# Later places in TensorE's order for the two products that spread v's maxima, and a place behind v's low parts for GpSimd's low parts of u

## The chip, the core and the metric

The kernel runs on one core of one Trainium2 chip. A core has five engines with a queue each, worked through in order: TensorE (PE, matrix products into PSUM), VectorE (DVE), ScalarE (ACT), GpSimd (POOL) and SyncE (SP), which issues the DMAs here. The metric is the device time of one execution, in microseconds (us).

## What is computed

Windowed attention, and behind it a mixing over tokens and over channels, on 8 batches of 8 heads, 576 tokens and 64 dimensions per head (512 channels):

```python
scores = scale * q @ k.T + bias          # only 0 <= i - j < 128
attn = exp(scores - max) / sum
x = attn @ v                             # heads side by side: (8, 576, 512)
theta = x @ w_theta
y = w_tok_r @ (x * cos(theta)) + w_tok_i @ (x * sin(theta))
u = x + y
out = u + maximum(u @ w_ch, 0)
```

## The kernel before, in words

Single numbers are carried as a high and a low part of smaller width, and a product is made of three products of parts. In TensorE's work this shows as groups like `wtk_hi,z_hi`, `wtk_lo,z_hi`, `wtk_hi,z_lo`.

**Two batches at a time.** After a start-up of its own, a loop over the batches runs `attend` for batch b+1 while the token mixing of batch b (`mix`, a generator that makes three products of 288 columns per step) fills TensorE in between; then `turn` transposes the new batch's x, multiplies by w_theta and makes z (cosine and sine), beside the channel products (`channels`) of batch b. `attend` is worked in four *slots* per batch, one per pair of heads; in the texts here slot 0 is the first. A slot p computes the scores of the next pair (`scores`, tiles `s_ps` and one `mm`; L394 on VectorE adds the bias and takes the extreme, L397 on ScalarE is the exponential), transposes the exponentials of its own pair (`flip`, four banks 0 to 3; tile `t_ps`; ScalarE copies the high part, L409, VectorE the low part, L410), multiplies them by v for its first head and its second (`values`, tile `acc`), and divides (`finish`, L444 to L447, into `x_sb`). Banks 0 and 2 are flipped at the slot's head, 1 and 3 behind the scores. STEPS (L33) gives the numbers of mixing steps put between them: 7, 7, 6, 3 in slot 0, 3, 4, 6, 4 in slot 1 and 3, 4, 6, 3 in slots 2 and 3.

**Buffers.** `t_ps` has two PSUM buffers, so flip 1 takes that of flip 0 and flip 3 that of flip 2, once ScalarE and VectorE have read them. `s_ps` and `acc` have one, `mm` has three, shared by the mixing, channel and theta products, the first score tile and the products of the change. `vh`/`vl` have two each.

**v's scales.** v is scaled by a power of two for each head before it is split. Heads are taken in groups of four. In an even slot `measure` takes the group's absolute maxima per partition (L239, then a floor, L241, into `peak`). In the next, odd, slot they are spread over the partitions: `spread_first` has TensorE transpose `peak` (L76), VectorE takes the maximum (L251) and makes a diagonal of it (L253); `spread_scales` has TensorE multiply ones by the diagonal (L71, `mm<-fixed`), and VectorE makes the scales (L127, L129; for every second group also the batch's scale, L268 to L270 and L134). `split_values` then uses a scale for a head: ScalarE makes `vh` (L329), GpSimd writes its ones column (L330), VectorE makes `vl` (L331). This is called by `ready` for the heads of the next pair, once behind the first head's `finish` and once behind the second's. `prepare` splits the next but one pair's q and k there too (`qh` L310, `ql` L311, `kh` L313 and `kl` on GpSimd L315) and issues the loads of the pair after that; `qr`, which they load, has one buffer, so its load follows `ql`.

**u's parts.** When a part of the mixing ends (eight parts per batch: a half of the tokens by a quarter of the channels), VectorE adds it to x (L567), ScalarE rounds it to `u_hi` (L569) and GpSimd makes the rest, `u_lo` (L570). The channel products read both.

**What sets the order.** From the main loop on, TensorE's instructions keep the order in which the program writes them (`pinned`). The other engines' orders are worked out ahead of time by the framework's scheduler, from its own estimate of times and from priorities; `high_priority(250)` moves the instructions of a block forward, and `issue_after(ins)` puts instructions behind another in that order. A semaphore wait is only put in where data or a buffer asks for it.

Of the kernel before, what the change touches and what calls it, by code (L numbers as in the profile page):

```python
# [34 lines left out]
GROUP = 4  # L35
# [11 lines left out]
def attn_moe_kernel(ctx: ExitStack, tc: tile.TileContext, qt, kt, vx, wth, wtok, wch, band, out):  # L47
# [19 lines left out]

    pinned = []

# [248 lines left out]
    def split_values(n):  # L318

        if n < H:  # L320
            if n % GROUP == 0:
                group_v[n // GROUP] = load_plain(n // GROUP)
            return (group_v[n // GROUP][:, n % GROUP],), None
        vb, scale = group_v[n // GROUP]
        k = n % GROUP
        v, vs = vb[:, k, :, :64], scale[:, k:k + 1]
        vh = vp.tile([128, 5, 65], F16, name="vh")
        vl = vp.tile([128, 5, 64], F16, name="vl")
        nc.scalar.activation(vh[:, :, :64], v, AF.Copy, scale=vs)  # L329
        nc.gpsimd.memset(vh[:, :, 64:], 1.0)  # L330
        nc.vector.scalar_tensor_tensor(out=vl, in0=v, scalar=vs, in1=vh[:, :, :64], op0=ALU.mult, op1=ALU.subtract)  # L331
        return (vh, vl), vs

# [84 lines left out]
    class Head:  # L418
# [5 lines left out]
        def ready(self):  # L424
            self.v, self.vs = split_values(self.n)

# [117 lines left out]
    def mix(st):  # L544
# [8 lines left out]
        def part(g, ks):  # L553
# [12 lines left out]
            if ks[-1] == 8:  # L566
                nc.vector.scalar_tensor_tensor(out=xtf[:, m, cs], in0=y_ps[:, :HALF], scalar=st["back"],  # L567
                                               in1=xtf[:, m, cs], op0=ALU.mult, op1=ALU.add)
                nc.scalar.copy(u_hi[:, m, cs], xtf[:, m, cs])  # L569
                nc.gpsimd.tensor_tensor(out=u_lo[:, m, cs], in0=xtf[:, m, cs], in1=u_hi[:, m, cs].bitcast(F32),  # L570
                                        op=ALU.subtract)
                yield
# [46 lines left out]
    def attend(b, x_sb, mixing, chans, first, behind):  # L619

        for g in range(H // 2):
# [18 lines left out]
            scores(SCORES[0])  # L640
            scores(SCORES[1])
            if scaled:
                with tc.high_priority(FINISH):
                    spread_first(scaled)
            step(mixing, steps[1])
            pair.flip(1)
            pair.flip(3)
            if scaled:
                with tc.high_priority(FINISH):
                    spread_scales(scaled)  # L650
            step(mixing, steps[2])
            one.values()
            with tc.high_priority(FINISH):
                done = one.finish(x_sb)
            scores(SCORES[2])
            with tc.issue_after(done.ins):
                if new is not None:
# [8 lines left out]
            if new is not None:  # L666
                with tc.issue_after(done.ins):
                    new.heads[1].ready()
                    if measured:
                        measure(measured)  # L670

    def start(x_sb, load):
# [140 lines left out]
```

## Time and profile before

| | us |
|---|---|
| three runs | 765.84, 770.71, 2267.97 (median 770.71) |
| the profiled execution | 762.94 |
| its span, first to last instruction | 761.2 |
| mean granted TensorE clock | 0.943 of full |

In the profile, a line such as L71 is that of the kernel above; since helpers record all matrix products, L71 holds nearly all of them, and L76 all transposes: the tiles tell them apart. A row of the timeline gives start, duration, engine, line, operation, output and inputs, shape and number, and in brackets the idle time of that engine just before with what ended it. A row of windows gives, per engine, busy time and number of instructions, then the granted clock of TensorE, the share of the DMA engines and GB/s. Matrix products overlap in the pipeline: the pace is read from start to start.

### The profile page before, as it was taken

To read this page: it belongs to the slowest core of one execution; us is meant where nothing else is said; L and a number is where in the kernel's file an instruction comes from. 1 tells how busy PE (TensorE), PEld (TensorE's weight loads), DVE (VectorE), ACT (ScalarE), POOL (GpSimd) and SP (SyncE) were. 2 spreads that over 40 slices of the span, in tenths; PEclk is the share of its full clock that TensorE was granted. 3 is DMA by queue.
4 is the path that set the end of the run, shared out by engine and by line. 5 is a ranking of instruction groups with operands and counts; after the bars stand their busy time and mean duration, and the time that the engine had idled before them with its cause. 6 is when DMAs were issued, how large, how long until landed. Compare 5 with 4: busy or idle time off the path is not lost.

```text
span 761.2 us, 16035 instructions
## 1 busy us (share of the span) xinstructions
PE 686.3 (90%) x6221; PEld 584.1 (77%) x6221; DVE 565.1 (74%) x1528; ACT 503.6 (66%) x988; POOL 156.5 (21%) x200
## 2 busy tenths in 40 slices
PE   4888797999979999799979999799989999799998
PEld 2567675789868888689868798688867898689887
DVE  6988756885887867886787867786687867874722
ACT  5988386576965678475966578565975579554910
POOL 2211321221221302221212302222211212210220
PEclk9886598999989999999999999899999999999999
DMA  9455200332021310232011220222012220000001
GB/s 304 149 182 181 78 1 1 89 85 64 24 67 33 93 57 14 67 103 68 24 53 47 81 65 17 67 76 88 23 42 66 75 71 17 18 9 33 25 9 55
DMA packets 32620, 49.86 MB, mean 66 GB/s; under 512 B 5664, under 2 KB 22048, under 8 KB 32544
## 3 DMA queue, kind: packets, MB, share of 16 engines
q1 hardware_dynamic: 32544, 48.84, 21.0%
q8 instruction: 49, 0.80, 0.4%
q14 instruction: 27, 0.22, 0.1%
HBM read 39.39 MB, written 9.44 MB: 64 GB/s over the span
## 4 chain that ended last, share of the span: by engine, by line
PE 44%; DVE 28%; ACT 21%; issue 3%; DMA 3%; SPq 1%; POOL 0%; DVEq 0%; ACTq 0%; POOLq 0%
PE mm L71 29%; PE acc L71 6%; PE t_ps L76 5%; DVE pt L410 4%; PE s_ps L71 3%; ACT g L509 3%; ACT z_hi L460 3%; ACT g L508 2%; DVE ql L311 2%; DVE peak L239 2%; ACT xtf L482 2%; DVE s_sb L394 2%; DVE g L513 2%; ACT x_hi L480 2%; DVE f L513 1%
## 5 line engine op out<-in xcount | busy, mean ns | idle before, releaser
L71 PE MATMUL mm<-wtk_hi,z_lo 128*128 128x288 f16 x576 | 169.9, 295 | 5.6 <-DVE z_lo L461 5.0
L71 PE MATMUL mm<-wtk_hi,z_hi 128*128 128x288 f16 x576 | 170.5, 296 | 3.8 <-ACT z_hi L460 3.8
L71 PE MATMUL mm<-wtk_lo,z_hi 128*128 128x288 f16 x576 | 170.0, 295 | 0.0
L397 ACT ACTIVATE s_sb<-s_sb,fixed 128x256 f32<-128x256 f32 (+1 forms) x256 | 104.1, 470 | 56.7 <-DVE fixed L394 56.7
L71 PEld LDWEIGHTS <-z_hi 128*128 128x128 f16 x1152 | 113.0, 102 | 36.6 <-ACT z_hi L460 4.4
L570 POOL TENSOR_TENSOR u_lo<-xtf,u_hi 128x288 fp32r<-128x288 f32 x64 | 50.6, 797 | 278.7 <-ACT u_hi L569 262.6
L410 DVE SCALAR_TENSOR_TENSOR pt<-t_ps,pt 128x512 f16<-128x512 f32 x112 | 74.7, 684 | 28.1 <-ACT pt L409 28.0
L394 DVE CUSTOM_DVE_ANT_0 s_sb<-s_ps,bands 128x256 f32<-128x256 f32 (+1 forms) x256 | 84.7, 384 | 1.2 <-PE s_ps L71 1.2
L71 PEld LDWEIGHTS <-z_lo 128*128 128x128 f16 x576 | 58.0, 101 | 26.1 <-DVE z_lo L461 8.6
L409 ACT ACTIVATE pt<-t_ps 128x512 f16<-128x512 f32 x112 | 61.6, 585 | 20.8 <-PE t_ps L76 20.8
L76 PE MATMUL t_ps<-fixed,s_sb 128*128 128x128 f32 x448 | 65.2, 286 | 4.5 <-ACT s_sb L397 2.3
L315 POOL TENSOR_TENSOR kl<-kr,kh 128x576 fp32r<-128x576 f32 x32 | 55.8, 1742 | 65.4 <-ACT kh L313 65.4
L569 ACT CAST u_hi<-xtf 128x288 fp32r<-128x288 f32 x64 | 27.2, 426 | 54.2 <-DVE xtf L567 53.7
L76 PEld LDWEIGHTS t_ps<-fixed,s_sb 128*128 128x128 f32 x448 | 55.0, 149 | 7.5 <-ACT s_sb L397 2.9
L71 PE MATMUL acc<-vh,pt 128*128 128x65 f16 x1008 | 55.8, 194 | 0.0
L71 PEld LDWEIGHTS <-pt 128*128 128x128 f16 x1512 | 52.8, 98 | 3.3
L71 PE MATMUL acc<-vl,pt 128*128 128x64 f16 x504 | 52.3, 193 | 0.0
L461 POOL TENSOR_TENSOR z_lo<-g,z_hi 128x512 f16<-128x512 f32 x16 | 19.1, 1196 | 156.1 <-ACT z_hi L460 156.1
L71 PE MATMUL s_ps<-kh,qh 64*128 64x256 f32 (+1 forms) x256 | 44.0, 341 | 7.3 <-DVE fixed L394 7.3
L71 PE MATMUL mm<-wth_hi,x_hi 128*128 128x512 f32 x160 | 48.0, 423 | 2.5 <-ACT x_hi L480 1.6
L567 DVE SCALAR_TENSOR_TENSOR xtf<-mm,fixed,xtf 128x288 f32<-128x288 f32 x64 | 32.3, 514 | 21.8 <-PE mm L71 21.2
L71 PE MATMUL mm<-u_hi,wch_hi 128*128 128x288 f32 x256 | 47.3, 307 | 0.0
(141 smaller groups left out, 1546.6 us busy)
## 6 DMA issues: line engine op xcount, KB each, us to landing
vb<-in_vx_dram SPq DMA_DIRECT2D x16, 650.0 KB, 5.2
kr<-in_kt_dram SPq DMA_DIRECT2D x32, 288.0 KB, 3.2
out_dram<-xtf SPq DMA_DIRECT2D x64, 144.0 KB, 1.8
qr<-in_qt_dram SPq DMA_DIRECT2D x32, 144.0 KB, 2.7
qr<-in_qt_dram SPq DMA_DIRECT2D x32, 128.0 KB, 2.8
xtf<-in_wtok_dram SPq DMA_DIRECT2D x4, 576.0 KB, 4.7
u_hi<-in_wtok_dram SPq DMA_DIRECT2D x3, 576.0 KB, 4.5
u_lo<-in_wtok_dram SPq DMA_DIRECT2D x2, 576.0 KB, 6.0
```

Of the source, the lines that this page charges most:

```text
L71: ins = nc.tensor.matmul(*args, **kw)
L76: ins = nc.tensor.transpose(*args)
L315: nc.gpsimd.tensor_tensor(out=kl, in0=kr, in1=kh.bitcast(F32), op=ALU.subtract)
L394: nc.vector.tensor_tensor_reduce(out=sb, in0=ps, in1=bias, scale=2.0 ** -(2 * self.p % H + 1), scalar=3.0e38, op0=ALU.add, op1=ALU.min, ac ...
L397: self.exp = nc.scalar.activation(sb, sb, AF.Exp, bias=least, scale=-1.0)
L409: nc.scalar.activation(pt[:, 0], t_ps, AF.Copy, scale=2.0 ** PEXP)
L410: nc.vector.scalar_tensor_tensor(out=pt[:, 1], in0=t_ps, scalar=2.0 ** PEXP, in1=pt[:, 0], op0=ALU.mult, op1=ALU.subtract)
L460: st["turned"] = nc.scalar.copy(z_hi[:, c, :], z)
L509: nc.scalar.activation(g[:n], g[:n], AF.Sin, bias=halfpi[:n], scale=-RAD)
L567: nc.vector.scalar_tensor_tensor(out=xtf[:, m, cs], in0=y_ps[:, :HALF], scalar=st["back"], in1=xtf[:, m, cs], op0=ALU.mult, op1=ALU.add)
L569: nc.scalar.copy(u_hi[:, m, cs], xtf[:, m, cs])
L570: nc.gpsimd.tensor_tensor(out=u_lo[:, m, cs], in0=xtf[:, m, cs], in1=u_hi[:, m, cs].bitcast(F32), op=ALU.subtract)
```

## The change

`spread_first` moves from behind the second scores to behind the third group of mixing steps, directly ahead of the first head's values, and `spread_scales` from behind the flips 1 and 3 to behind the slot's last scores. `ready` hands back the instruction that makes `vl`, and the subtraction that makes `u_lo` is kept in a list for all batches but the last and written at the end of the slot, in a block behind the second head's `vl`. No instruction is added or removed.

```diff
-    pinned = []
+    pinned, lows = [], []
...
-        nc.vector.scalar_tensor_tensor(out=vl, in0=v, scalar=vs, in1=vh[:, :, :64], op0=ALU.mult, op1=ALU.subtract)
-        return (vh, vl), vs
+        low = nc.vector.scalar_tensor_tensor(out=vl, in0=v, scalar=vs, in1=vh[:, :, :64], op0=ALU.mult,
+                                             op1=ALU.subtract)
+        return (vh, vl), vs, low
...
         def ready(self):
-            self.v, self.vs = split_values(self.n)
+            self.v, self.vs, low = split_values(self.n)
+            return low
...
                 nc.scalar.copy(u_hi[:, m, cs], xtf[:, m, cs])
-                nc.gpsimd.tensor_tensor(out=u_lo[:, m, cs], in0=xtf[:, m, cs], in1=u_hi[:, m, cs].bitcast(F32),
-                                        op=ALU.subtract)
+                def low(m=m, cs=cs):
+                    nc.gpsimd.tensor_tensor(out=u_lo[:, m, cs], in0=xtf[:, m, cs], in1=u_hi[:, m, cs].bitcast(F32),
+                                            op=ALU.subtract)
+
+                if st["b"] + 1 < B:
+                    lows.append(low)
+                else:
+                    low()
...
             scores(SCORES[1])
+            step(mixing, steps[1])
+            pair.flip(1)
+            pair.flip(3)
+            step(mixing, steps[2])
             if scaled:
                 with tc.high_priority(FINISH):
                     spread_first(scaled)
-            step(mixing, steps[1])
-            pair.flip(1)
-            pair.flip(3)
-            if scaled:
-                with tc.high_priority(FINISH):
-                    spread_scales(scaled)
-            step(mixing, steps[2])
             one.values()
             with tc.high_priority(FINISH):
                 done = one.finish(x_sb)
             scores(SCORES[2])
+            if scaled:
+                with tc.high_priority(FINISH):
+                    spread_scales(scaled)
             with tc.issue_after(done.ins):
                 if new is not None:
                     new.heads[0].ready()
...
                 with tc.issue_after(done.ins):
-                    new.heads[1].ready()
+                    done = new.heads[1].ready()
+                    with tc.issue_after(done.ins):
+                        for low in lows:
+                            low()
                     if measured:
                         measure(measured)
+            else:
+                for low in lows:
+                    low()
+            lows.clear()
```

The rows below are the program's order on an engine, with the semaphores that an instruction waits for in brackets (named for the engine that raises them). TensorE in a slot 1 of the steady state, before, from the last scores of the next pair's second group (`peak_108` is the tile of maxima, `z_hi` the mixing's weights):

```order
L71 MATMUL s_ps<-kh,ql 128x256 x2
L71 MATMUL s_ps<-kl,qh 128x256 x2
L76 MATMUL mm<-fixed,peak_108 128x128 [waits DVE_49]
L71 LDWEIGHTS z_hi
L71 MATMUL mm<-wtk_hi,z_hi 128x288
L71 LDWEIGHTS z_hi
L71 MATMUL mm<-wtk_lo,z_hi 128x288
L71 LDWEIGHTS z_lo
L71 MATMUL mm<-wtk_hi,z_lo 128x288
```

The transpose of the maxima stands directly behind the scores, ahead of the mixing. There, now, the slot runs on into the mixing and the flips of banks 1 and 3 (`t_ps`):

```order
L71 LDWEIGHTS z_lo
L71 MATMUL mm<-wtk_hi,z_lo 128x288
L76 MATMUL t_ps<-fixed,s_sb_3804 128x128 [waits DVE_49]
L76 MATMUL t_ps<-fixed,s_sb_3804 128x128
L76 MATMUL t_ps<-fixed,s_sb_3804 128x128 [waits Activation_49]
L76 MATMUL t_ps<-fixed,s_sb_3804 128x128
L76 MATMUL t_ps<-fixed,s_sb_3805 128x128 [waits DVE_49,PE_49]
L76 MATMUL t_ps<-fixed,s_sb_3805 128x128
L76 MATMUL t_ps<-fixed,s_sb_3805 128x128 [waits Activation_49]
L76 MATMUL t_ps<-fixed,s_sb_3805 128x128
L71 LDWEIGHTS z_hi
```

The transpose is gone from here, and the flips themselves now wait for VectorE, which they did not have to do behind a transpose that waited for it. It now stands ahead of the first head's values, and the product with the diagonal behind the last scores:

```order
L71 LDWEIGHTS z_lo
L71 MATMUL mm<-wtk_hi,z_lo 128x288
L76 MATMUL mm<-fixed,peak_108 128x128 [waits DVE_49]
L71 LDWEIGHTS pt [waits Activation_49]
L71 MATMUL acc<-vh,pt 128x65 [waits Pool_49]
L71 LDWEIGHTS pt
```

It is the last TensorE instruction ahead of `acc`. Further on in the same slot, behind the second head's score products:

```order
L71 MATMUL s_ps<-kh,ql 128x256 x2
L71 MATMUL s_ps<-kl,qh 128x256 x2
L71 MATMUL mm<-fixed 128x4 [waits DVE_49]
L71 LDWEIGHTS z_hi
L71 MATMUL mm<-wtk_hi,z_hi 128x288
L71 LDWEIGHTS z_hi
```

Both keep their wait for VectorE. ScalarE at the end of the same slot, before and then now (`vh` is v's high part for the next pair, `pt` the high part of a flip of the next slot):

```order
L329 ACTIVATE vh<-vb,fixed 128x5x64 [waits PE_49,DMAHW3_49,Activation_49,Pool_49]
L313 CAST kh<-kr 128x576 [waits DMAHW2_49,PE_49]
L397 ACTIVATE s_sb_4046<-s_sb_4046,fixed 128x256 [waits DVE_49]
L397 ACTIVATE s_sb_4047<-s_sb_4047,fixed 128x256 [waits DVE_49]
L397 ACTIVATE s_sb_4046<-s_sb_4046,fixed 128x256 [waits DVE_49]
L329 ACTIVATE vh<-vb,fixed 128x5x64 [waits PE_49,Activation_49,Pool_49]
L397 ACTIVATE s_sb_4047<-s_sb_4047,fixed 128x256 [waits DVE_49]
L409 ACTIVATE pt<-t_ps 128x512 [waits PE_49]
L409 ACTIVATE pt<-t_ps 128x512 [waits PE_49,Activation_49]
L310 ACTIVATE qh<-qr,fixed 128x640 [waits DMAHW6_49,DMAHW5_49,DMAHW4_49]
```

There one `vh` stood ahead of `kh` and the other among the exponentials. Now:

```order
L313 CAST kh<-kr 128x576 [waits DMAHW2_49,PE_49]
L398 ACTIVATE s_sb_4036<-s_sb_4036,fixed 128x256 [waits DVE_49]
L398 ACTIVATE s_sb_4037<-s_sb_4037,fixed 128x256 [waits DVE_49]
L398 ACTIVATE s_sb_4036<-s_sb_4036,fixed 128x256 [waits DVE_49]
L398 ACTIVATE s_sb_4037<-s_sb_4037,fixed 128x256 [waits DVE_49]
L329 ACTIVATE vh<-vb,fixed 128x5x64 [waits DVE_49,DMAHW3_49,Activation_49,Pool_49]
L329 ACTIVATE vh<-vb,fixed 128x5x64 [waits PE_49,Activation_49,Pool_49]
L410 ACTIVATE pt<-t_ps 128x512 [waits PE_49]
L310 ACTIVATE qh<-qr,fixed 128x640 [waits DMAHW6_49,DMAHW5_49,DMAHW4_49]
L410 ACTIVATE pt<-t_ps 128x512 [waits PE_49,Activation_49]
```

Both `vh` stand together now behind the four exponentials, the first of them waits for VectorE's scale, and `qh` stands between the two `pt`. VectorE at the end of slot 3, before and then now (the row with `x_hi` belongs to `turn`):

```order
L567 SCALAR_TENSOR_TENSOR xtf<-mm,fixed,xtf 128x288 [waits PE_49]
L593 SCALAR_TENSOR_TENSOR xtf<-mm,xtf 128x288 [waits PE_49,Pool_49]
L444 TENSOR_SCALAR fixed<-acc,fixed 128x5 [waits PE_49]
L446 RECIPROCAL fixed<-fixed 128x5 [waits DVE_49]
L447 TENSOR_TENSOR x_sb<-acc,fixed 128x5x64 [waits DVE_49]
L331 SCALAR_TENSOR_TENSOR vl<-vb,fixed,vh 128x320 [waits Activation_49]
L593 SCALAR_TENSOR_TENSOR xtf<-mm,xtf 128x288 [waits PE_49,Pool_49]
L476 TENSOR_TENSOR x_hi<-t_ps,x_hi 128x4x64 [waits Activation_49]
```

The second head's end stood behind the two `xtf` sums. Now:

```order
L569 SCALAR_TENSOR_TENSOR xtf<-mm,fixed,xtf 128x288 [waits PE_49]
L129 TENSOR_SCALAR fixed<-fixed 128x4 [waits DVE_49]
L601 SCALAR_TENSOR_TENSOR xtf<-mm,xtf 128x288 [waits PE_49,Pool_49]
L331 SCALAR_TENSOR_TENSOR vl<-vb,fixed,vh 128x320 [waits Activation_49]
L446 TENSOR_SCALAR fixed<-acc,fixed 128x5 [waits PE_49]
L448 RECIPROCAL fixed<-fixed 128x5 [waits DVE_49]
L449 TENSOR_TENSOR x_sb<-acc,fixed 128x5x64 [waits DVE_49]
L331 SCALAR_TENSOR_TENSOR vl<-vb,fixed,vh 128x320 [waits Activation_49]
L601 SCALAR_TENSOR_TENSOR xtf<-mm,xtf 128x288 [waits PE_49,Pool_49]
L478 TENSOR_TENSOR x_hi<-t_ps,x_hi 128x4x64 [waits Activation_49]
```

A `vl` and the last step of the scale (L129) have come in ahead of the second head's end, the three rows of L444 to L447 (now L446 to L449). GpSimd at the end of slot 3, before and then now (`kl` is k's low part):

```order
L570 TENSOR_TENSOR u_lo<-xtf,u_hi 128x288 [waits Activation_49] x2
L330 MEMSET vh 128x5 [waits PE_49,Pool_49]
L315 TENSOR_TENSOR kl<-kr,kh 128x576 [waits DMAHW1_49,PE_49,Activation_49]
L330 MEMSET vh 128x5 [waits PE_49,Pool_49]
L570 TENSOR_TENSOR u_lo<-xtf,u_hi 128x288 [waits Activation_49]
```

The last `u_lo` of the batch closed the row. Now:

```order
L573 TENSOR_TENSOR u_lo<-xtf,u_hi 128x288 [waits Activation_49] x2
L330 MEMSET vh 128x5 [waits PE_49,Pool_49]
L315 TENSOR_TENSOR kl<-kr,kh 128x576 [waits DMAHW1_49,PE_49,Activation_49]
L573 TENSOR_TENSOR u_lo<-xtf,u_hi 128x288 [waits Activation_49]
L330 MEMSET vh 128x5 [waits PE_49,Pool_49]
```

The last `u_lo` stands ahead of the memset instead of behind it. And GpSimd in the slots 0 and 1 that follow, before and then now:

```order
L570 TENSOR_TENSOR u_lo<-xtf,u_hi 128x288 [waits Activation_49,Pool_49]
L570 TENSOR_TENSOR u_lo<-xtf,u_hi 128x288 [waits Activation_49]
L330 MEMSET vh 128x5 [waits PE_49]
L315 TENSOR_TENSOR kl<-kr,kh 128x576 [waits DMAHW7_49,PE_49,Activation_49]
L330 MEMSET vh 128x5 [waits PE_49]
L570 TENSOR_TENSOR u_lo<-xtf,u_hi 128x288 [waits Activation_49]
L330 MEMSET vh 128x5 [waits PE_49,Pool_49]
L570 TENSOR_TENSOR u_lo<-xtf,u_hi 128x288 [waits Activation_49]
L315 TENSOR_TENSOR kl<-kr,kh 128x576 [waits DMAHW2_49,PE_49,Activation_49]
```

Two `u_lo` lead, and one follows each of two memsets. Now:

```order
L573 TENSOR_TENSOR u_lo<-xtf,u_hi 128x288 [waits Activation_49,Pool_49]
L573 TENSOR_TENSOR u_lo<-xtf,u_hi 128x288 [waits Activation_49]
L330 MEMSET vh 128x5 [waits PE_49]
L315 TENSOR_TENSOR kl<-kr,kh 128x576 [waits DMAHW7_49,PE_49,Activation_49]
L330 MEMSET vh 128x5 [waits PE_49,Pool_49]
L573 TENSOR_TENSOR u_lo<-xtf,u_hi 128x288 [waits Activation_49]
L330 MEMSET vh 128x5 [waits PE_49,Pool_49]
L573 TENSOR_TENSOR u_lo<-xtf,u_hi 128x288 [waits Activation_49]
L315 TENSOR_TENSOR kl<-kr,kh 128x576 [waits DMAHW2_49,PE_49,Activation_49]
```

These stand as they stood, and `u_lo` waits for ScalarE (and the first for GpSimd itself), not for VectorE.

More of the change, by code (lines that the diff above doesn't have):

```diff
@@ L322, in split_values @@
                 group_v[n // GROUP] = load_plain(n // GROUP)
-            return (group_v[n // GROUP][:, n % GROUP],), None
+            return (group_v[n // GROUP][:, n % GROUP],), None, None
         vb, scale = group_v[n // GROUP]
```

## The prediction

> **What bounds the kernel now.** I read the page first, then the waits, the timeline of one batch, and busy time by windows. From the page, the span and the engines' busy shares:
>
> ```profile
> span 761.2 us, 16035 instructions
> PE 686.3 (90%) x6221; PEld 584.1 (77%) x6221; DVE 565.1 (74%) x1528; ACT 503.6 (66%) x988; POOL 156.5 (21%) x200
> ```
>
> TensorE is nearly always busy, so what counts is why it idles and how fast it is clocked. From the waits (us in total, times, longest):
>
> ```profile
> PE mm L76 <- DVE peak L241: 30.1, 13, 3.3
> PE s_ps L71 <- DVE fixed L394: 7.3, 8, 1.7
> ```
>
> The largest wait is the first of the two products to be moved: 13 times TensorE stands at the transpose of the maxima until VectorE has measured them. The timeline at the start of slot 1 (I number a batch's slots 0 to 3; 1 and 3 spread maxima), then the stall in the first such slot and in a slot 3:
>
> ```profile
> 309.23 0.28 PE L71 MATMUL s_ps<-kl,qh 64*128 64x256 f32 x2
> 309.30 0.54 DVE L331 SCALAR_TENSOR_TENSOR vl<-vb,fixed,vh 128x320 f16<-128x320 f32 x1
> 309.76 1.48 DVE L239 TENSOR_REDUCE peak<-vb 128x4 f32<-128x1280 f32 x1
> 311.16 0.68 DVE L410 SCALAR_TENSOR_TENSOR pt<-t_ps,pt 128x512 f16<-128x512 f32 x1
> 312.03 0.69 DVE L410 SCALAR_TENSOR_TENSOR pt<-t_ps,pt 128x512 f16<-128x512 f32 x1
> 312.63 0.16 DVE L241 TENSOR_SCALAR peak<-peak 128x4 f32<-128x4 f32 x1
> 312.85 0.33 PE L76 MATMUL mm<-fixed,peak 128*128 128x128 f32 x1 [3.34 <-DVE peak L241]
> ...
> 139.09 0.47 PE L76 MATMUL mm<-fixed,peak 128*128 128x128 f32 x1 [1.85 <-DVE peak L241]
> ...
> 341.47 0.33 PE L76 MATMUL mm<-fixed,peak 128*128 128x128 f32 x1 [1.30 <-DVE peak L241]
> ```
>
> Of the 13 waits, six are of the 3.34 kind (20.0 us), one is the 1.85, six are of slot 3 (30.1 - 20.0 - 1.85 = 8.2). Behind each slot-1 stall the granted clock (the column after POOL) is halved; I took the seven windows in which it stood at half, first, third and sum shown, and one behind a slot-3 stall:
>
> ```profile
> 139.00:142.40 3.40, 3.31 (x14) 2.21 (x15) 1.98 (x12) 1.92 (x5) 0.79 (x1) 0.50 0.29 107
> ...
> 313.10:316.50 3.40, 3.40 (x17) 2.42 (x16) 1.56 (x9) 1.85 (x5) 0.80 (x1) 0.50 0.16 55
> ...
> sum 30.00, PE 27.22 PEld 19.90 DVE 15.72 ACT 16.74 POOL 5.32; mean PE 3.89 PEld 2.84 DVE 2.25 ACT 2.39 POOL 0.76
> ...
> 341.50:344.90 3.40, 3.40 (x30) 2.97 (x31) 2.57 (x13) 2.65 (x7) 0.16 (x1) 1.00 0.29 106
> ```
>
> 27.22 us of TensorE work at half clock would take half as long at full clock: 13.6 us lost, 1.7 of it in the first slot 1 (half of 3.31), 2.0 in each of the other six. So the stalls and their clock cost 43.7 us, the most that this change could return.
>
> **The change: part one, the products.** Nothing is added or removed. In a scaled slot the transpose moves behind 12 mixing products, eight flips and up to 18 more mixing products; the product with the diagonal moves behind the first head's values and the last scores.
>
> *Start of slot 1.* TensorE is free at 309.23 + 0.28 = 309.51. The pace of mixing products and the flips of a slot that does not spread:
>
> ```profile
> 338.45 0.29 PE L71 MATMUL mm<-wtk_hi,z_hi 128*128 128x288 f16 x1
> 338.57 0.29 PE L71 MATMUL mm<-wtk_lo,z_hi 128*128 128x288 f16 x1
> ...
> 328.28 1.04 PE L76 MATMUL t_ps<-fixed,s_sb 128*128 128x128 f32 x8
> 331.36 0.19 PE L71 MATMUL acc<-vh,pt 128*128 128x65 f16 x1
> ```
>
> Twelve at 0.12 end at 310.98. Then comes the wait that stood hidden under the old one: flip 1 takes the buffer of flip 0, which VectorE's low part reads until 311.84, and flip 3 that of flip 2, until 312.72. So 0.86 us and, four transposes (0.45) later, 0.43: 1.29 instead of 3.34, a gain of 2.05. In the first slot 1 the same steps find both parts done; 1.85 goes entirely.
>
> *Clock.* The 1.3 us left are no longer than the slot-3 stalls, behind which the clock is 1.00. I take the full 2.0 (1.7 in the first). The other end is 0, since 1.85 us did halve it.
>
> The Trainium skill (TensorE: Matmul & The Clock Gate, "What's actually happening") has the clock halve after at least one idle window of some 3.4 us. Here the halving after 1.85 us of idleness disagrees with that; by the page alone these stalls, all shorter, would not be what halves it, and the sum would lose its clock term.
>
> *Middle of slot 1.* Flips and 18 products last 331.36 - 328.28 = 3.08, so the transpose comes at about 315.5 and the first head's values end at 316.5. The diagonal's product needs L251 and L253, which on VectorE now stand behind both low parts (0.68 each) and a part of u's columns:
>
> ```profile
> L567 DVE SCALAR_TENSOR_TENSOR xtf<-mm,fixed,xtf 128x288 f32<-128x288 f32 x64 | 32.3, 514 | 21.8 <-PE mm L71 21.2
> ...
> L251 DVE TENSOR_REDUCE fixed<-mm 128x1 f32<-128x128 f32 x15 | 4.3, 285 | 0.0
> ```
>
> I put the end of flip 3's low part at 316.2 to 316.3 (ScalarE makes its high part behind four exponentials), and then 0.51, 0.29 and as much again for L253: 317.3. TensorE reaches the product after the last scores, near 317.4. About level: I take no wait; ends 0 and 0.3 a batch.
>
> *End of slot 1.* The spread values now arrive late, so ScalarE's vh and VectorE's vl of the first head stand behind the second head, directly ahead of the low parts that release the next slot's flips; on ScalarE the second flip's high part now stands behind qh, which waits for its DMA. Against that, VectorE loses an idle time and a collision:
>
> ```profile
> 302.00:328.28 26.28, 22.20 (x263) 18.57 (x259) 22.43 (x66) 14.77 (x31) 6.55 (x10) 0.94 0.24 71
> ...
> 317.35 0.16 DVE L127 TENSOR_SCALAR fixed<-mm 128x4 int32<-128x4 int32 x1 [2.69 <-PE mm L71]
> 321.29 0.88 DVE L311 SCALAR_TENSOR_TENSOR ql<-qr,fixed,qh 128x640 fp32r<-128x640 f32 x1
> 322.08 1.70 DVE L331 SCALAR_TENSOR_TENSOR vl<-vb,fixed,vh 128x320 f16<-128x320 f32 x1
> ...
> 321.94 1.49 POOL L315 TENSOR_TENSOR kl<-kr,kh 128x576 fp32r<-128x576 f32 x1 [0.50 <-ACT kh L313]
> ...
> 305.10 2.03 DVE L311 SCALAR_TENSOR_TENSOR ql<-qr,fixed,qh 128x640 fp32r<-128x640 f32 x1
> ...
> 304.82 1.62 POOL L315 TENSOR_TENSOR kl<-kr,kh 128x576 fp32r<-128x576 f32 x1
> ```
>
> vl beside GpSimd's kl took 1.70 against 0.54 alone; ql begun before kl 0.88, begun after it 2.03. vl now stands clear of kl. But kh no longer waits behind vh, so kl can start about when ql does. If ql is first, VectorE runs 3.7 us earlier at the end of the slot and the next flips do not wait: the 2.05 and the clock's 1.7 to 2.0 are kept. If kl is first, ql loses 1.15, qh's DMA starts that much later, and the flips of slot 2 wait 1.15. My steps put the two within 0.1 us, less than their error, so I take the middle: 0.6 lost.
>
> The Trainium skill (SBUF — State Buffer, "Who interferes with whom") says that a VectorE instruction with two SBUF inputs and a GpSimd one that reads SBUF exclude each other for a whole instruction, whichever starts first; the rows of ql agree, and by it the loss is either nothing or the whole 1.15.
>
> *Slot 3.* TensorE is free 1.30 before 341.47, runs 12 products to 341.65, and the low parts of the flips were done at 340.46 and 341.34 (first two rows below). All of 8.2 is regained. But vl of the first head now stands ahead of the second head's end, which the next stage waits for:
>
> ```profile
> 339.77 0.69 DVE L410 SCALAR_TENSOR_TENSOR pt<-t_ps,pt 128x512 f16<-128x512 f32 x1
> ...
> 340.65 0.69 DVE L410 SCALAR_TENSOR_TENSOR pt<-t_ps,pt 128x512 f16<-128x512 f32 x1
> ...
> 351.57 0.41 ACT L569 CAST u_hi<-xtf 128x288 fp32r<-128x288 f32 x1
> ...
> 351.88 0.22 DVE L444 TENSOR_SCALAR fixed<-acc,fixed 128x5 f32<-128x5 f32 x1
> ...
> 352.36 0.49 DVE L447 TENSOR_TENSOR x_sb<-acc,fixed 128x320 f32<-128x320 f32 x1
> ...
> 353.35 0.60 PE L76 MATMUL t_ps<-fixed,x_sb 128*128 128x128 f32 x4
> ...
> 353.68 0.84 ACT L310 ACTIVATE qh<-qr,fixed 128x640 fp32r<-128x640 f32 x1 [1.16 <-DMA qr<-in_qt_dram]
> ...
> 380.56 0.30 PE L71 MATMUL mm<-wtk_hi,z_lo 128*128 128x288 f16 x1 [0.66 <-DVE z_lo L461]
> ```
>
> x_sb ended at 352.85, 0.5 ahead of TensorE; the head's end (L444) began at 351.88. Now vh starts behind u_hi on ScalarE, which ends about 0.5 before its old 351.98 (the queues ahead lost a vl), so vh is done near 352.1, vl near 352.6 (352.85 if it meets u_lo on GpSimd), and only then comes L444: 0.75 to 1.0 later, 0.25 to 0.5 of waiting. ScalarE also has one more vh, behind qh, ahead of x_hi, and that stage already ends with TensorE waiting 0.66 for it. I take 0.6 in each of six batches; ends 0 and 1.2.
>
> **Part two, GpSimd's low parts of u.** The instructions that the order shows carry no new wait: u_lo still waits for ScalarE alone and stands where it stood, but for one place in slot 3, where it goes ahead of a small memset. So vl of slot 0 will meet u_lo as before, and I cost this part at nothing. Ends: nothing, and 0.6 per batch if it did wait (vl of slot 0 back from 1.12 to 0.54):
>
> ```profile
> 303.27 1.55 POOL L570 TENSOR_TENSOR u_lo<-xtf,u_hi 128x288 fp32r<-128x288 f32 x2 [12.82 <-ACT u_hi L569]
> ...
> 304.05 1.12 DVE L331 SCALAR_TENSOR_TENSOR vl<-vb,fixed,vh 128x320 f16<-128x320 f32 x1
> ```
>
> SP's queue is not reordered; qr's loads follow ql, as said. The vectors of the first group and the last batch are untouched.
>
> **The sum,** against the profiled execution (762.9 us, span 761.2 and 1.7 around it): slot 1, six times 2.05 + 2.0 - 0.6 = 20.7; the first one 1.85 + 1.7 = 3.5; slot 3 gives 8.2 - 3.6 = 4.6. Together 28.8: 734. The runs shown, 765.8 and 770.7, lie 3 and 8 above the profiled one; I take the nearer and predict 737.
>
> **Rivals.**
> 1. *The clock stays gated.* 0.86 and 0.43 us of waiting in one stretch, added to a wait of s_ps before them (7.3 us in 8), might still halve it. Against: 1.00 behind 1.30. The clock term's 13.7 goes: 751. The page's rule gives the same time by another way: windows that these stalls do not cause stay. Chance 0.10.
> 2. *VectorE and ScalarE become the bound.* VectorE is busy 22.43 of 26.28 us in slots 0 and 1; my steps ask it for some 3.7 less. If kl is always first and qh's DMA holds back the high part, each batch keeps about 2.5 us less: 745 to 750. Chance 0.15.
> 3. *The waits re-form so far that little remains*, flips and the next stage both late: 755 to 768. Against: VectorE's idle 2.69 in the old slot shows room. Chance 0.11.
> 4. *GpSimd does wait as the words say:* six times 0.6 more, 733. The order speaks against it. Chance 0.06.
> 5. *Slower, by the diagonal's product.* TensorE's queue is fixed, so a late L253 stops everything. It decides once L253 lies some 5 us behind TensorE in slot 1 (28.8 over six), with the clock halved again: six times 7.5 against 28.8 is 16 slower, 782. My steps have them level. Chance 0.03.
>
> **How the numbers follow.** My forecast, 727 (kl second, no loss at the next stage) to 742, has 0.55. The range 726 to 753 holds it and rivals 1, 2 and 4 and leaves out rivals 3 and 5 and some of the tails, together under 0.2. A measurement of this kernel tells about 2%, here 15 us, from no change: faster needs less than 755. Forecast and rivals 1, 2, 4 are below it with small tails: 0.82; rival 3 and the tails 0.14; slower 0.04.
>
> **What would show it.** The wait of L76 for peak gone, TensorE's largest new waits at t_ps in slot 1 at about 0.9 and 0.4; no half-clock window in the steady batches; vl in slot 1 at 0.54; vl in slot 0 still near 1.12 with u_lo beside it; x_sb later against TensorE at the end of slot 3. A wait at the diagonal's product above 1 us, half-clock windows, or flips of slot 2 that wait over 1.2 would prove me wrong.

## The result, and the profile after

The changed kernel takes 732.1 us (median of four runs, 731.1 to 733.2) against 770.7: a ratio of 0.952, 95% interval 0.947 to 0.957. One run of the kernel before took 2268 us; the ratio and its interval leave it out. The profiled execution took 731.1 against 762.9, which is 31.8 less; 28.8 less had been forecast. From the page of the changed kernel, and its waits (us in total, times, longest), those of TensorE that the loop has:

```profile
span 729.2 us, 16045 instructions
PE 678.5 (93%) x6219; PEld 578.7 (79%) x6221; DVE 556.5 (76%) x1528; ACT 500.2 (69%) x988; POOL 155.9 (21%) x200
```

```profile
PE s_ps L71 <- DVE fixed L395: 7.3, 8, 1.7
PE t_ps L76 <- DVE pt L411: 5.6, 8, 0.8
PE mm L71 <- DVE z_lo L463: 5.0, 8, 0.7
...
PE t_ps L76 <- DVE peak L241: 2.2, 7, 0.3
```

The wait for the maxima, 30.1 us in 13 times before, is gone. In its place stand the two waits at t_ps, 7.8 together; those at s_ps and z_lo are old. The timeline of the steady slot 1, of the changed kernel (start, duration, engine, line):

```profile
299.52 1.48 DVE L239 TENSOR_REDUCE peak<-vb 128x4 f32<-128x1280 f32 x1
300.92 0.68 DVE L411 SCALAR_TENSOR_TENSOR pt<-t_ps,pt 128x512 f16<-128x512 f32 x1
...
301.65 0.66 PE L76 MATMUL t_ps<-fixed,s_sb 128*128 128x128 f32 x4 [0.80 <-DVE pt L411]
301.79 0.68 DVE L411 SCALAR_TENSOR_TENSOR pt<-t_ps,pt 128x512 f16<-128x512 f32 x1
302.62 0.63 PE L76 MATMUL t_ps<-fixed,s_sb 128*128 128x128 f32 x4 [0.31 <-DVE peak L241]
...
305.29 0.27 PE L76 MATMUL mm<-fixed,peak 128*128 128x128 f32 x1
...
307.21 0.38 PE L71 MATMUL mm<-fixed 128*128 128x4 f32 x2
...
307.64 0.88 DVE L311 SCALAR_TENSOR_TENSOR ql<-qr,fixed,qh 128x640 fp32r<-128x640 f32 x1
307.96 1.82 POOL L315 TENSOR_TENSOR kl<-kr,kh 128x576 fp32r<-128x576 f32 x1 [0.23 <-ACT kh L313]
311.41 1.00 DVE L331 SCALAR_TENSOR_TENSOR vl<-vb,fixed,vh 128x320 f16<-128x320 f32 x2
```

Neither moved product waits. Flips 1 and 3 wait 0.80 and 0.31 where 0.86 and 0.43 were forecast. (For the second the profile names L241, the floor of the maxima; what flip 3 needs by the program is the low part of flip 2, which ended at 302.47, 0.15 ahead of it.) ql starts 0.32 ahead of kl and takes 0.88; the two vl, 1.00 together, are clear of kl.

Where the time came from is read from windows cut at TensorE's first transpose of x_sb in each batch's turn: up to the first, up to the second, the six batches behind it, and the end. First the kernel before, then the changed one (length, then busy time of PE, PEld, DVE, ACT, POOL; the column behind POOL is the granted clock):

```profile
0.00:75.62 75.62, 54.93 (x346) 40.80 (x346) 64.53 (x206) 59.39 (x121) 13.58 (x20) 0.83 0.63 206
75.62:179.48 103.86, 89.23 (x767) 73.80 (x768) 78.20 (x211) 64.61 (x128) 25.34 (x29) 0.84 0.18 51
179.48:694.37 514.89, 479.35 (x4664) 415.30 (x4663) 394.51 (x1064) 352.29 (x692) 106.65 (x139) 0.97 0.18 52
694.37:761.10 66.73, 62.79 (x450) 54.18 (x448) 27.91 (x48) 27.29 (x49) 10.89 (x12) 0.99 0.09 32
```

```profile
0.00:76.25 76.25, 58.03 (x344) 43.80 (x346) 65.10 (x206) 59.13 (x121) 14.07 (x20) 0.78 0.62 204
76.25:174.94 98.69, 87.12 (x767) 72.77 (x768) 76.26 (x210) 64.38 (x128) 25.17 (x29) 0.86 0.19 55
174.94:662.48 487.54, 470.58 (x4665) 407.95 (x4663) 387.24 (x1066) 349.38 (x692) 105.81 (x139) 1.00 0.19 55
662.48:729.20 66.72, 62.79 (x450) 54.17 (x448) 27.88 (x48) 27.29 (x49) 10.87 (x12) 1.00 0.10 32
```

| | length | TensorE's idle | TensorE's own work |
|---|---|---|---|
| start-up | +0.63 | | |
| first batch | -5.17 | -3.06 | -2.11 |
| six batches | -27.35 | -18.58 | -8.77 |
| end | -0.01 | | |

So TensorE idles 21.6 us less, and works through the same products in 10.9 us less: the clock in the six batches is at 1.00 and was at 0.97.

### The profile page after: what moved, and what is told of

The parts are those of the page before. It is cut to its first block, busy times and chain, and to the rows that moved or that the text cites. A ratio compares the mean times of both kernels' runs of the same rounds, so it can differ in the third digit from the quotient of the medians.

```text
span 729.2 us, 16045 instructions
## 1 busy us (share of the span) xinstructions
PE 678.5 (93%) x6219; PEld 578.7 (79%) x6221; DVE 556.5 (76%) x1528; ACT 500.2 (69%) x988; POOL 155.9 (21%) x200
## 4 chain that ended last, share of the span: by engine, by line
PE 44%; DVE 25%; ACT 23%; issue 3%; DMA 3%; SPq 1%; POOL 0%; ACTq 0%; DVEq 0%; POOLq 0%
PE mm L71 28%; PE acc L71 6%; PE t_ps L76 5%; PE s_ps L71 4%; DVE pt L411 4%; ACT g L511 3%; ACT z_hi L462 3%; ACT g L510 3%; DVE ql L311 2%; ACT xtf L484 2%; DVE s_sb L395 2%; DVE g L515 2%; ACT x_hi L482 2%; DVE f L515 2%; ACT s_sb L398 1%
## 5 line engine op out<-in xcount | busy, mean ns | idle before, releaser
L71 PE MATMUL mm<-wtk_hi,z_lo 128*128 128x288 f16 x576 | 165.3, 287 | 5.6 <-DVE z_lo L463 5.0
L71 PE MATMUL mm<-wtk_hi,z_hi 128*128 128x288 f16 x576 | 165.7, 288 | 3.9 <-ACT z_hi L462 3.9
L71 PE MATMUL mm<-wtk_lo,z_hi 128*128 128x288 f16 x576 | 165.2, 287 | 0.0
L71 PEld LDWEIGHTS <-z_hi 128*128 128x128 f16 x1152 | 109.1, 99 | 33.5 <-ACT z_hi L462 4.4
L71 PEld LDWEIGHTS <-z_lo 128*128 128x128 f16 x576 | 56.4, 98 | 24.2 <-DVE z_lo L463 9.2
L76 PEld LDWEIGHTS t_ps<-fixed,s_sb 128*128 128x128 f32 x448 | 51.9, 145 | 16.9 <-DVE pt L411 6.8
```

Of the source, the lines that this page charges most:

```text
L71: ins = nc.tensor.matmul(*args, **kw)
L76: ins = nc.tensor.transpose(*args)
```

## The experiments

In each diff, lines with - are the kernel named. Times are medians of four runs; the kernel before, run on the same chips beside them, had medians of 767.5 to 768.5. Ratios are to it, with a 95% interval.

**1. Part one alone.** Against the changed kernel:

```diff
-                if st["b"] + 1 < B:
-                    lows.append(low)
-                else:
-                    low()
+                low()
```

> Part one alone: the two products at their new places, GpSimd's low parts of u written at once as before the change. My theory: part two of the change puts no wait and no new order on GpSimd (a queueing rule between instructions of two different engines binds neither), so this is the changed kernel, 732 +- 2 us, vl of slot 0 still 1.12 us beside u_lo. Rival (GpSimd does wait as the words say, worth 0.6 us in each of six batches): 3.5 us slower than the changed kernel, 735 or more.

731.1 us, ratio 0.953 [0.950, 0.956]. The order of the instructions on all five engines, with the semaphores that they wait for, is that of the changed kernel, buffer numbers aside. So part two as written does nothing, and the one `u_lo` that changed its place in slot 3 did so by part one: `issue_after(done.ins)` names an instruction of VectorE, and no instruction of GpSimd was put behind it. The kernel queues kl behind ql by the same rule, and in slot 0 kl starts 0.27 us ahead of ql all the same (rows under experiment 5).

**2. The clock without the stall's cover.** Against the kernel before, in slots 1 only:

```diff
-    def spread_from(peak, n, part):
+    def spread_from(peak, n, part, k=0):
         m_ps = ps_m.tile([128, 512], F32, name="mm")
+        for _ in range(k):
+            mm(m_ps[:, 128:384], ident.bitcast(BF16)[:, :128], bnd.bitcast(BF16)[:, :256], start=True, stop=True)
         flipped(m_ps[:, :128], peak, ident)
...
-                    spread_first(scaled)
+                    spread_first(scaled, 20 if g == 1 else 0)
```

> The kernel before the change, but 20 small products without inputs from VectorE (128 columns by 256, into columns of the bank that nobody reads) stand directly ahead of the transpose in every slot 1: they last about 2.2 us (a product of 288 columns takes 0.123), so the work behind the stall starts no sooner, but TensorE idles 1.1 us in place of 3.34. My theory (the half clock behind the stall comes from TensorE's idleness, and is worth 1.7 + 6 x 2.0 = 13.6 us by itself): no half-clock window in the loop and about 13 us less than before, 757. Rival (the clock falls for another reason, or costs nothing because TensorE is not the bound there): the windows stay, or go without a gain, 768 to 773.

757.5 us, ratio 0.986 [0.983, 0.990]. From the timeline of this kernel, the fillers and the stall behind them, and a slot 3; then windows behind the one and the other, and the six batches:

```profile
309.79 2.36 PE L71 MATMUL mm<-bands,fixed 128*128 128x256 bf16 x20
313.19 0.33 PE L76 MATMUL mm<-fixed,peak 128*128 128x128 f32 x1 [1.04 <-DVE peak L241]
...
254.09 0.34 PE L76 MATMUL mm<-fixed,peak 128*128 128x128 f32 x1 [1.93 <-DVE peak L241]
```

```profile
180.91:688.30 507.39, 484.74 (x4784) 421.33 (x4783) 394.56 (x1064) 352.14 (x692) 106.74 (x139) 0.99 0.18 53
313.30:316.70 3.40, 3.40 (x31) 2.94 (x31) 2.47 (x13) 2.91 (x7) 0.80 (x1) 1.00 0.16 58
254.30:257.70 3.40, 3.40 (x16) 2.41 (x15) 1.61 (x9) 1.46 (x4) 0.00 (x0) 0.50 0.06 21
```

As much time is lost ahead of the transpose (2.36 of filler and 1.04 of wait, 3.40 against the old 3.34), but TensorE is busy for most of it, and all seven stretches of half clock behind the stalls of slots 1 go. Two new windows of half clock came behind stalls of slots 3, which were 1.93 and 2.15 there; before they were 1.27 to 1.79. Why these two grew was not followed. The six batches are 7.5 shorter than before. The two new windows cost 1.7 each (half of 3.40), and the stalls of slots 3 were 0.9 longer in all (7.9 against 7.0), which makes 11.8 for the clock of slots 1. I had put 12.0 for these six. The half clock comes from idleness, and costs about what half of TensorE's work in the window says.

**3. The transpose ahead of the flips.** Against the changed kernel:

```diff
             step(mixing, steps[1])
+            if scaled:
+                with tc.high_priority(FINISH):
+                    spread_first(scaled)
             pair.flip(1)
             pair.flip(3)
             step(mixing, steps[2])
-            if scaled:
-                with tc.high_priority(FINISH):
-                    spread_first(scaled)
```

> The changed kernel, but the transpose of the maxima stands behind the 12 mixing products only, ahead of flips 1 and 3. In the steady slots 1 TensorE must wait 3.34 - 1.47 = 1.87 us there, and the flips then wait no more: 0.76 us longer than the 1.11 of the changed kernel, 4.6 us over six batches. Theory A (a stall of 1.85 us is enough to halve the clock, as in the first slot 1 of the kernel before): half-clock windows in the six steady slots 1, 2.0 each, 732 + 4.6 + 12 = 749. Theory B (1.85 us alone was not what did it): clock at full, 737. If only the stalls counted and not the place behind the flips, the same 737.

735.6 us, ratio 0.958 [0.954, 0.962]: the time and the clock are those of theory B. The stall and the window behind it:

```profile
308.62 0.33 PE L76 MATMUL mm<-fixed,peak 128*128 128x128 f32 x1 [1.75 <-DVE peak L241]
```

```profile
308.70:312.10 3.40, 3.40 (x35) 2.95 (x36) 3.14 (x14) 2.77 (x7) 0.45 (x1) 1.00 0.23 81
```

Six stalls of 1.75 or 1.76, six times a full clock. So the flips need not be passed to save the clock; twelve mixing products are enough, with at most 0.1 us to spare by the table of the last section. That the 1.85 of the first slot 1 was not what halved the clock does not follow, since the stall here came out shorter than the 1.87 expected.

**4. The diagonal's product close behind.** Against the changed kernel:

```diff
                     spread_first(scaled)
+                    spread_scales(scaled)
             one.values()
...
             scores(SCORES[2])
-            if scaled:
-                with tc.high_priority(FINISH):
-                    spread_scales(scaled)
```

> The changed kernel, but the product with the diagonal directly behind the transpose of the maxima, both ahead of the first head's values. It prices the second move. My theory: L251 and L253 cannot be hidden, TensorE waits for them about 1.0 us (0.29 + 0.28 + 0.23 and the hand-overs), and up to 1.7 where VectorE is in a low part of a flip, in each of 13 slots: 13 to 20 us slower than the changed kernel, 745 to 752, clock at full. Rival (the first move does all the work, the earlier scales give vh and vl back their early places and pay for the wait): within 4 us of the changed kernel.

746.2 us, ratio 0.972 [0.969, 0.976], 14 slower than the changed kernel. From the timeline, slot 1 and slot 3:

```profile
311.25 0.27 PE L71 MATMUL mm<-fixed 128*128 128x4 f32 x1 [1.34 <-DVE fixed L253]
...
339.01 0.27 PE L71 MATMUL mm<-fixed 128*128 128x4 f32 x1 [0.94 <-DVE fixed L253]
```

TensorE waits 1.34 in each slot 1, 0.65 or 0.94 in each slot 3. The second move is worth over a third of the whole change; in the changed kernel the product comes 1.92 behind the transpose (305.29 to 307.21 above) and finds L253 done.

**5. Part two made to bind.** Against the changed kernel; the new instruction runs on GpSimd and reads one column of vl:

```diff
+    tok = const.tile([128, 2], F16, name="tok")
+
+    def behind_of(t):
+        return nc.gpsimd.tensor_tensor(out=tok[:, :1], in0=ones, in1=t, op=ALU.subtract)
...
-                    with tc.issue_after(done.ins):
-                        for low in lows:
-                            low()
+                    if lows:
+                        with tc.issue_after(behind_of(new.heads[1].v[1][:, 0, :1]).ins):
+                            for low in lows:
+                                low()
```

> The changed kernel, but GpSimd's low parts of u truly wait as the words of the change say: a one-column GpSimd instruction that reads the second head's vl stands ahead of them in GpSimd's queue. It asks what part two would have been worth. My theory: in slot 0 vl falls from 1.12 to 0.54, ql then starts ahead of kl and takes 0.88 in place of 2.03, so VectorE is 1.73 us earlier: the 0.74 at s_ps and most of the 0.81 and 0.31 at t_ps go, 1.5 to 1.85 us in each of six batches, 9 to 11 less than the changed kernel, 721 to 723. The lower end as forecast for rival 4: vl alone, 0.6 each, 3.5 less, 728. Rival (the low parts now run later beside x_lo and z_lo at the turn and lengthen them): no gain or a loss, 732 or more.

722.0 us, ratio 0.940 [0.938, 0.942]: faster than both kernels. Slot 0 of the changed kernel, then of this one:

```profile
293.04 1.55 POOL L573 TENSOR_TENSOR u_lo<-xtf,u_hi 128x288 fp32r<-128x288 f32 x2 [12.81 <-ACT u_hi L571]
293.82 1.12 DVE L331 SCALAR_TENSOR_TENSOR vl<-vb,fixed,vh 128x320 f16<-128x320 f32 x1
294.59 1.62 POOL L315 TENSOR_TENSOR kl<-kr,kh 128x576 fp32r<-128x576 f32 x1
294.86 2.03 DVE L311 SCALAR_TENSOR_TENSOR ql<-qr,fixed,qh 128x640 fp32r<-128x640 f32 x1
298.32 0.33 PE L71 MATMUL s_ps<-kh,qh 64*128 64x128 f32 x2 [0.74 <-DVE fixed L395]
```

```profile
293.47 0.55 DVE L336 SCALAR_TENSOR_TENSOR vl<-vb,fixed,vh 128x320 f16<-128x320 f32 x1
293.94 0.88 DVE L316 SCALAR_TENSOR_TENSOR ql<-qr,fixed,qh 128x640 fp32r<-128x640 f32 x1
294.08 2.02 POOL L320 TENSOR_TENSOR kl<-kr,kh 128x576 fp32r<-128x576 f32 x1 [1.86 <-ACT kh L318]
297.69 0.19 POOL L94 TENSOR_TENSOR tok<-fixed,vl 128x1 f16<-128x1 f32 x1 [1.52 <-DVE vl L336]
297.83 1.55 POOL L578 TENSOR_TENSOR u_lo<-xtf,u_hi 128x288 fp32r<-128x288 f32 x2
```

This is a chain: without u_lo beside it vl is 0.57 shorter, so ql starts 0.14 ahead of kl and not 0.27 behind it, and takes 0.88 and not 2.03. The one that comes second pays: kl is now 2.02. TensorE's wait at s_ps is gone; of those at t_ps the 0.31 stays, and two batches have one of 0.44 and 0.68 in slot 2. The six batches:

```profile
176.24:653.51 477.27, 469.25 (x4664) 407.93 (x4663) 375.90 (x1065) 348.91 (x693) 113.97 (x165) 1.00 0.19 56
```

TensorE idles 8.0 us in place of 17.0.

**6. The same in slot 0 alone.** Against experiment 5:

```diff
-                        with tc.issue_after(behind_of(new.heads[1].v[1][:, 0, :1]).ins):
+                        with tc.issue_after(behind_of(new.heads[1].v[1][:, 0, :1]).ins) if g == 0 else nullcontext():
```

> The changed kernel with the true wait of GpSimd's low parts of u for the second head's vl in slot 0 of each batch alone; in slots 1 to 3 they run at once. My theory: what the wait gave (722 against 732) is the meeting of vl with u_lo and of ql with kl in slot 0, so all of it comes from there: 722 +- 2. Rival (the other slots' vl and ql share in it): 726 or more.

722.3 us, ratio 0.941 [0.938, 0.944], the same as with the wait in every slot: all of the gain comes from slot 0.

**7. kl behind ql.** Against the changed kernel:

```diff
-        with tc.issue_after(low.ins) if pinned else nullcontext():
+        with tc.issue_after(behind_of(ql.bitcast(F32)[:, :1]).ins) if pinned else nullcontext():
             nc.gpsimd.tensor_tensor(out=kl, in0=kr, in1=kh.bitcast(F32), op=ALU.subtract)
```

> The changed kernel, but kl truly waits for ql in every slot: a one-column GpSimd instruction that reads ql stands directly ahead of kl. My theory: in slot 0 ql takes 0.88 in place of 2.03, VectorE is 1.15 earlier, the 0.74 at s_ps goes and 0.41 of the 1.12 at t_ps: 1.15 in each of six batches, 7 less than the changed kernel, 725. vl of slot 0 stays at 1.12. Rival (kl, now later, meets the next two-input instructions of VectorE, and the time only moves): 732 +- 2.

729.2 us, ratio 0.949 [0.947, 0.951]: 3 less than the changed kernel, not 7. ql is 0.88 in every slot and the wait at s_ps is gone; two batches wait 0.79 and 1.00 at t_ps in slot 2, and others 0.3 at the diagonal's product. What ties these to the later kl was not tried. In the profiled executions the six batches are 4.3 shorter, and 2.2 of that is lost again in a longer start-up, which this edit does not reach.

**8. The measurement behind the low part of flip 2.** Against the changed kernel; `flip` hands back the instruction of its low part:

```diff
             pair.flip(0)
-            pair.flip(2)
+            low = pair.flip(2)
+            if scaled:
+                with tc.issue_after(low.ins):
+                    measure(scaled)
...
-                    if measured:
-                        measure(measured)
```

> The changed kernel, but VectorE measures the maxima (L239, 1.48 us) behind the low part of flip 2 in slots 1 and 3, not ahead of that of flip 0. My theory: the 0.81 and 0.31 that TensorE waits at t_ps in the steady slots 1 come from that measurement alone; both go, 1.1 in each of six batches, 6 to 7 less than the changed kernel, 725, and the transpose of the maxima, 3.6 us behind flip 1, still finds them ready. Rival (the measurement now delays the low parts of flips 1 and 3 and so the first head's values): a wait of up to 1.5 there, 732 to 738.

744.5 us, ratio 0.969 [0.966, 0.971]: 12 slower than the changed kernel, outside what either theory gave. Slot 1 and the start of slot 2:

```profile
303.00 1.48 DVE L239 TENSOR_REDUCE peak<-vb 128x4 f32<-128x1280 f32 x1
306.00 1.50 DVE L411 SCALAR_TENSOR_TENSOR pt<-t_ps,pt 128x512 f16<-128x512 f32 x2
309.19 2.11 DVE L311 SCALAR_TENSOR_TENSOR ql<-qr,fixed,qh 128x640 fp32r<-128x640 f32 x1
...
316.14 0.83 ACT L310 ACTIVATE qh<-qr,fixed 128x640 fp32r<-128x640 f32 x1 [1.37 <-DMA qr<-in_qt_dram]
...
318.32 0.63 PE L76 MATMUL t_ps<-fixed,s_sb 128*128 128x128 f32 x4 [1.81 <-DVE pt L411]
```

The 0.80 at flip 1 did go (0.31 is left). But flips 1 and 3's low parts are late, and so ql, which now finds kl ahead of it and takes 2.11; the DMA into qr, which waits for ql, is late; qh waits for it, and the low part of the next flip behind qh. That is the course of rival 2 of the prediction, "kl is always first and qh's DMA holds back the high part", set off by 1.5 us on VectorE. At the turn x_sb is late too: TensorE waits for it in six places, 4.9 us in all, against one of 1.0 in the changed kernel.

**9. Experiments 7 and 8 together.**

> kl behind ql, and the measurement behind the low part of flip 2, together in the changed kernel. My theory: 0.74 at s_ps and 1.12 at t_ps all go, 1.85 in each of six batches, 11 less than the changed kernel, 721. If the two gains are the same idle time seen twice: 725.

732.3 us, ratio 0.954 [0.952, 0.957]. With kl held behind ql the measurement's move costs 3 (against experiment 7) and not 12, but it gains nothing.

**10. Part two, binding, without part one.** Against experiment 5, the two products are back at their old places.

> The kernel before the change with the true wait of GpSimd's low parts of u in every slot, and both products of the maxima at their old places: part two alone, made to bind. My theory: VectorE is 1.73 us earlier in slot 0, of which 0.74 goes at s_ps and the rest shortens the stall at the transpose from 3.34 to about 2.35: 1.7 in each of six batches, 10 less than before, 758; the half-clock windows stay, since 2.35 is above the 1.85 that halved the clock. Rival A (with the stall shorter the clock stays full too): 10 more, 748. Rival B (the wait is worth something only behind the moved products): 768.

750.3 us, ratio 0.978 [0.973, 0.982]: 18 less than before, between my theory and rival A. The stall of the steady slots 1 fell to 2.4, as forecast; half of their stretches of half clock went too. Two stalls and what lies behind each:

```profile
227.96 0.33 PE L76 MATMUL mm<-fixed,peak 128*128 128x128 f32 x1 [2.42 <-DVE peak L246]
...
396.94 0.33 PE L76 MATMUL mm<-fixed,peak 128*128 128x128 f32 x1 [2.40 <-DVE peak L246]
```

```profile
228.60:232.00 3.40, 3.40 (x17) 2.76 (x15) 1.17 (x7) 1.85 (x5) 0.00 (x0) 0.50 0.07 27
397.00:400.40 3.40, 3.40 (x30) 2.96 (x31) 2.38 (x13) 3.01 (x7) 0.00 (x0) 1.00 0.18 66
```

Equal stalls, and only three of the six halved the clock. The last section says on what it depends.

**11. Both true waits on GpSimd.** Experiments 5 and 7 together.

> The changed kernel with both true waits on GpSimd: low parts of u behind the second head's vl, kl behind ql. My theory: with the first of them ql already runs alone in slots 0 and 1, so the second adds nothing: 722 +- 1.5. Rival (the waits of 0.44 and 0.68 at t_ps that are left in slot 2 of two batches come from kl beside ql): 720 or less. Rival (kl, held back, meets vl or the measurement): 724 or more.

724.9 us, ratio 0.945 [0.942, 0.949]: 3 more than experiment 5 alone. The idle of the six batches went from 8.0 to 10.2. As in experiment 7, holding kl back costs something where nothing is left to gain.

## Why the prediction was right

737 was forecast and 732.1 measured. The sum missed by 3.0 (28.8 against 31.8 in the profiled executions); the other 2 are the runs, which lie 1.0 above the profiled execution now and had been put 3 above it. The mechanism came as described, and the size is in part luck: TensorE's idle time fell by 6.4 more than the sum had it, its own work by 2.8 less. Point by point:

*The stall* was right: the wait for the maxima is gone, 1.11 is left at the flips in each steady slot 1 (1.29 forecast), and a few of 0.3 to 0.4 in slots 2 and 3.

*The clock* was right in kind: no half window, and experiment 2 measures it alone at 11.8 us for six batches (12.0 forecast). In the changed kernel TensorE's own work shrank by 8.8 there. Most of the rest stands in the transposes of the scores, which took, from start to start, 39.2 us in the six batches, no less than before (39.1), against 36.8 in experiment 3, where the flips come later. Short waits that the rows count as work would look like this; it is not settled. Rival 1 did not come: the fullest window of the steady loop held 1.12 us of idle time, which is the two waits at the flips. The 0.74 at s_ps ends 2.5 us ahead of them and lies in another window, and the last section puts the limit near 1.8.

*"I take the middle: 0.6 lost"* was mis-sized. ql comes first in every slot 1 (six ql of 2.03 in the loop, all in slots 0), and nothing is lost there, against 3.6 us in the sum. Experiment 8 shows that the other branch was real; ql is ahead by about 0.3 us only.

*"I take 0.6 in each of six batches"* at the turn was mis-sized too, by the 3.6 us of the sum. From the timeline after:

```profile
336.27 0.42 ACT L571 CAST u_hi<-xtf 128x288 fp32r<-128x288 f32 x1
336.59 0.56 ACT L329 ACTIVATE vh<-vb,fixed 128x320 f16<-128x320 f32 x1
337.19 0.73 DVE L331 SCALAR_TENSOR_TENSOR vl<-vb,fixed,vh 128x320 f16<-128x320 f32 x1 [0.21 <-ACT vh L329]
337.84 0.21 DVE L446 TENSOR_SCALAR fixed<-acc,fixed 128x5 f32<-128x5 f32 x1
338.31 0.49 DVE L449 TENSOR_TENSOR x_sb<-acc,fixed 128x320 f32<-128x320 f32 x1
...
338.74 0.60 PE L76 MATMUL t_ps<-fixed,x_sb 128*128 128x128 f32 x4
```

vl does stand ahead of the head's end and meets u_lo (0.73). But u_hi ended 2.05 ahead of TensorE's transpose of x_sb, 1.37 before; I had put the gain at 0.5. The head's end lost 0.57 against TensorE (0.90 ahead of the transpose, 1.47 before), not the 0.75 to 1.0 forecast. And the margin was larger than the 0.5 that I had read from the first of the four transposes: only the fourth, 0.33 behind the first, needs the pair of heads that has just ended. It alone of the four waits for a semaphore, and in experiment 8 the wait at the turn stands ahead of it (1.12 us in this batch). From the end of x_sb to the fourth transpose it was 0.82 before the change and is 0.27 now (338.80 to 339.07), so TensorE does not wait. Only one batch has a wait at this stage (0.75, at x_hi).

*Start-up* was 0.63 longer, with more of it at half clock (0.78 against 0.83); I had not counted it, and the change does not touch it. In the thirteen profiled executions it lasts from 75.2 to 80.4 us though no edit reaches it, so a few us between two single executions can lie there. Idle 21.6 less and own work 10.9 less, minus 0.6: 31.9 in the span. The forecast had 15.2 and 13.7.

*Part two* at nothing: right, by the same order as without it. But rival 4's price, 0.6 a batch, was too small by a factor of three: I counted vl and not ql behind it, whose race with kl the 0.57 decides. Made to bind, part two gives 10 us.

*Rival 5*, the diagonal's product, has experiment 4 for a price: 14 us if it stands too near.

## What to carry to other kernels

A stall of the engine that bounds a kernel can cost again behind itself; here nearly a third of the stalls' cost by the prediction's reckoning (13.6 of 43.7 us) was the clock, experiment 2 bears out 11.8 of the 12.0 that it puts on six batches, and filling the stall with useless work won 10 us. Where two engines hold each other up, look at who starts first: 0.14 to 0.3 us of order decided 1.15 us, and the consequences ran on through a DMA into the next slot. An ordering rule in the source is worth what stands in the engines' queues: part two read well and changed no instruction, while one instruction of 0.19 us per batch on the right engine gained 10 us (experiment 6).

## What the runs showed of the hardware

The granted clock is set anew on a fixed grid: in the clock record of each of the thirteen traces every change lies a whole multiple of 3.413 us behind the first. How much TensorE idled within one window of that grid goes with the clock of the next, so a stall's place on it counts. I laid the grid of each trace's clock record over TensorE's idle times, for the loops of all of them. Idle time within one window that began at full clock, and the next window:

| idle in the window, us | next window |
|---|---|
| 1.84, 1.93, 2.13, 2.15, 2.18, 2.42 and six from 2.46 to 3.19 | half |
| 1.74 (the first slot 1 before; 0.11 more lies just beyond the edge) | half |
| 1.81, 1.79, three of 1.76, 1.75, 1.65, 1.60 and all below | full |

The limit lies near 1.8, a little over half a window; as the row of 1.74 shows, it is known to about 0.1. In experiment 10 the stalls of 2.4 that fell across an edge (1.34 and 1.31 idle in the fuller window of two of them, 1.81 in the third) left the clock alone; those of which 2.13 to 2.42 lay in one window did not. No run moved a stall along the grid by intent: this is read from where the stalls happened to fall. A half-clock window with 0.73 or 1.46 us of idle was followed by another, one with 0.51 or less by a full one.

The Trainium skill (TensorE: Matmul & The Clock Gate, "What's actually happening") describes a free-running window of about 3.4 us, and these traces agree. The same section of the Trainium skill has the clock halve after at least one idle window; here windows that were idle for 54% of their length did it.

Of VectorE and GpSimd, whichever came second paid: ql 0.88 or 2.03 to 2.11, kl 1.41 when ql had ended and 2.02 when begun behind it (experiments 7 and 5), vl 0.54 alone and 0.73, 1.12 or 1.70 beside u_lo or kl. In all three of these cases vl ended 0.34 to 0.35 behind the instruction it had met (u_lo at 337.58 and vl at 337.92 in the turn, 294.59 and 294.94 in slot 0; kl at 323.43 and vl at 323.78 before the change), so all but 0.2 us of its 0.54 came behind that.
